# Attention numerators in fp32 column halves, with the last stage written in a new order

## The chip, the cores and the metric

The kernel runs on one core of one Trainium2 chip. The metric is the device time of one execution in microseconds (us). The kernel before takes 759.59 us (median of 3 runs, 759.57 to 759.64).

## The reference

Two branches see the same 2048 rows of x (640 wide): a linear attention with 32 heads of 20 columns, and a feed-forward. A sigmoid gate mixes them row by row.

```
pq, pk = q @ w_phi, k @ w_phi                    # per head
phi = concat(softmax(p), softmax(-p))            # 40 features a head
kv  = phi_k^T v ;  z = sum of phi_k              # over all 2048 rows
num = phi_q kv  ;  den = phi_q z + 1e-6          # per query row and head
a   = concat over heads of (num / den) @ wo
b   = silu(x @ w1) @ w2
out = g * a + (1 - g) * b ,  g = sigmoid(x . gate_w)
```

## The kernel before

The work stands in three stages. The first builds keys, values and the sums kv and z. The second is the feed-forward in four blocks of 512 rows, whose gated result goes to DRAM (`fb_d`). The last stage is the attention of the queries, for eight pairs of query tiles of 128 rows; pairs are numbered by u in the order of the list `PB`.

**Numbers in two parts.** Most products are made in fp32r, a form of fp32 that TensorE takes in one pass at reduced precision. An operand is split into a high part (copy, by ScalarE) and a low part (difference, by VectorE or GpSimd), and a product is three matmuls: high by high, high by low, low by high (`PASSES`).

**One pair of query tiles** goes through these steps; the names are those of the functions.

- `q_mm`: the projection of one tile of 128 queries, 30 matmuls into a PSUM pair `pq`.
- `q_max`, `q_sub` (VectorE): maximum and minimum of each head, and the differences to them, four instructions. `q_exp` (ScalarE): the exponential. `q_sum` (VectorE): the softmax sums. `q_norm` (GpSimd): the product `ez` with z. `q_norm_sum`, `q_small` (VectorE): denominators and the weights of each head. `q_mul` (GpSimd): the features times these weights.
- `t_mm`: the features of both tiles are transposed, in six parts i of 0 to 5, into PSUM tiles `pT`; 22 instructions a pair. `t_hi` (ScalarE) and `t_lo` (VectorE) split each part into `fT`.
- `n_mm`: the numerators, part by part, into PSUM tiles `pn`. Part i holds two groups of three heads (120 features each; part 5 holds the last two heads). Their kv weights lie in `kvw`, 60 columns used of 120, the even group in the left half, the odd in the right, zeros elsewhere; so both groups add up into the same 120 rows of `pn`. Three passes and two groups make 6 matmuls a part, 3 for part 5, 33 a pair. `n_hi` and `n_lo` split `pn` into `oT`.
- `w_mm`: the product with wo, in three turns (two blocks of 128 output columns, two, one) of 16 matmuls a block, into PSUM tiles `pa`. `w_copy` (ScalarE) empties `pa`, `w_add` (GpSimd) adds the feed-forward's part, and a DMA writes it out.

`x_next(k)` prepares k more pieces of x for later projections: ScalarE makes the high part (`xb` from `xrb`), GpSimd the low part. There are three pieces to a pair (512, 512 and 256 columns).

`pT`, `pn` and `pa` share four PSUM tiles in turn (`single`), twelve uses a pair, so each use waits for the reader of the fourth use before it.

**Order.** In the last stage every engine runs its instructions in the order in which the code writes them (`inorder`). `step(u)` for u of 1 to 5 works on pair u, on the projections of two later tiles, b = 2u-1 and c = 2u, and on the wo product of pair u-1. The tile a = 2u-2 is the c of the step before. `last_steps(6)` ends the work. In before, the steps of one pair are interleaved finely: transposes and numerators of single parts alternate, and parts of the wo product stand between them.

Of the kernel before, what the change touches and what calls it, by code (L numbers as in the profile page):

```python
# [30 lines left out]
GW = GR * DH  # L31
NG = H // GR
# [30 lines left out]
def mix_kernel(ctx: ExitStack, tc: tile.TileContext, xT, wqT, wkc, wkr, wv, bd, bdc, cst, wo, w1, w1r, w2, out):  # L63
# [212 lines left out]
    vs = [ta.tile([P, KG, P], F32R, name=f"v{k}")[:, :, :VW] for k in range(VB)]  # L276
# [453 lines left out]
    def wo_load(c):  # L730
        wor_raw[c] = r = raw(f"wo{c}")
        nc.sync.dma_start(r[:GW, :D], wo[c * GW : (c + 1) * GW, :])

    def wo_split(c):
        r = wor_raw.pop(c)
        split(WO[:GW, c, 0], WO[:GW, c, 1], r[:GW, :D])
# [152 lines left out]
    def make_kvw():  # L889

        parts = [w.rearrange("p j f -> p (j f)").rearrange("p (i q f) -> p i q f", q=4, f=KD) for w in kvw]
        for h in range(2):
            nc.gpsimd.memset(parts[h][:, :, 1:3].bitcast(F32), 0.0)  # L893
        pts = []
        for j0, n in ((0, 8), (8, 3)):
            pt = bank(f"pkvt{j0}")
            pts.append((j0, n, pt))
            for j in range(j0, j0 + n):
                w = min(KF, 2 * D - j * KF)
                nc.tensor.transpose(  # L900
                    pt[:w, (j - j0) * KD : (j - j0 + 1) * KD], kvb["kvm"][:, j * KF : j * KF + w], ident[:KD, :KD]
                )
        yield
        for j0, n, pt in pts:
            n = min(n, 2 * NG - j0)
            i0, i1 = j0 // 2, (j0 + n) // 2
            split(
                *(part[:, i0:i1, ::3] for part in parts),
                pt[:GW, : n * KD].rearrange("p (i a f) -> p i a f", a=2, f=KD),
            )  # L910
        split(
            *(kvwr[:, h].rearrange("p (k f) -> p k f", f=REST) for h in range(2)),
            pt[:RC, None, n * KD : n * KD + REST].to_broadcast([RC, KH, REST]),
        )
        yield

    def kvw_of(h, j):
        return kvw[h][:, j, :] if j < 2 * NG else kvwr[:, h, :]

# [77 lines left out]
    def t_hi(u, i):  # L997
        pT = fTs[u, i]
        nj, w = (2, GW) if i < NG else (1, RC)
        if (u, i) < (0, 4):  # L1000
            f = slot(f"fT{u}_{i}")
        else:
            f = slot(f"fT{u}_{i}", fu, "u", 3) if i % 2 == 0 else slot(f"fT{u}_{i}", tb, "fT", 2)
        nc.scalar.copy(f[:w, 0, : nj * 256], pT[:w, : nj * 256])
        fTs[u, i] = f, pT

    def t_lo(u, i):
        f, pT = fTs[u, i]
        nj, w = (2, GW) if i < NG else (1, RC)
        nc.vector.tensor_tensor(  # L1010
            f[:w, 1, : nj * 256], pT[:w, : nj * 256], f[:w, 0, : nj * 256].bitcast(F32), op=ALU.subtract
        )
        fTs[u, i] = f
# [4 lines left out]
    with inorder(PE, DVE, ACT, POOL):  # L1018
# [34 lines left out]
        kvw = [wslot(f"kvw{h}", F32R)[:GW, : 2 * NG * GW].rearrange("p (j f) -> p j f", f=GW) for h in range(2)]  # L1053
        kvwr = fu.tile([RC, 2, GW], F32R, name="kvwr")
# [40 lines left out]
        for i in range(4):  # L1095
            t_mm(0, i, bank)
            t_hi(0, i)
            t_lo(0, i)
# [17 lines left out]
    for k in range(3):  # L1116
        nc.sync.dma_start(wor[k * REST : (k + 1) * REST, :D], wo[NG * GW :, :])

    def n_mm(u, gp, a):
        if (gp, a) == (0, 0):  # L1120
            oTs[u] = tb.tile([GW, 2, NG + 1, 256], F32R, tag="oT", name=f"oT{u}", bufs=2)
# [3 lines left out]
        nj, w = (2, GW) if i < NG else (1, RC)  # L1125
        f = fTs.pop((u, i))
        n = 0
        for jj in range(nj):
            for hk, hp in PASSES:
                nc.tensor.matmul(  # L1130
                    pns[u, gp][:GW, a, :],
                    kvw_of(hk, 2 * i + jj)[:w],
                    f[:w, hp, jj * 256 : (jj + 1) * 256],
                    start=(n == 0),
                    stop=(n == 3 * nj - 1),
                )
                n += 1
# [3 lines left out]
    def n_hi(u, gp):  # L1141
        o, pn = oTs[u], pns[u, gp]
        if gp < 2:
            nc.scalar.copy(o[:, 0, 2 * gp : 2 * gp + 2, :], pn[:GW])
        else:
            nc.scalar.copy(o[:, 0, 4, :], pn[:GW, 0])
            nc.scalar.activation(o[:, 1, 5, :], pn[:GW, 1], AF.Copy, scale=stk[:GW, 0:1])

    def n_lo(u, gp):
        o, pn = oTs[u], pns.pop((u, gp))  # L1150
        k = slice(2 * gp, 2 * gp + 2) if gp < 2 else slice(4, 5)
        nc.vector.tensor_tensor(o[:, 1, k, :], pn[:GW, : k.stop - k.start], o[:, 0, k, :].bitcast(F32), op=ALU.subtract)
        if gp == 2:
            nc.vector.scalar_tensor_tensor(
                o[:, 0, 5, :], pn[:GW, 1], stk[:GW, 1:2], o[:, 1, 5, :].bitcast(F32), op0=ALU.mult, op1=ALU.add
# [4 lines left out]
    def w_mm(u, m0, n):  # L1160
# [9 lines left out]
        for a in range(n):  # L1170
            ds = slice((m0 + a) * P, (m0 + a + 1) * P)
            for k, (c, ho, hw) in enumerate(todo):
                nc.tensor.matmul(  # L1173
                    pa[:, a, :],
                    WO[:GW, c, hw, ds] if c < NG else WOR[:, ds],
                    o[:, ho, c, :],
# [47 lines left out]
    def n_last(u):  # L1224
        n_mm(u, 2, 0)
        n_mm(u, 2, 1)
        n_hi(u, 2)

    def t_pair(u, i):
        for k in (i, i + 1):  # L1230
            t_mm(u, k)
        for k in (i, i + 1):
            t_hi(u, k)

    def n_first(u):
        n_mm(u, 0, 0)
        t_mm(u, 2)
        t_hi(u, 2)
        n_mm(u, 0, 1)
        t_mm(u, 3)  # L1240
        n_hi(u, 0)
        t_hi(u, 3)

    def n_second(u):
        n_mm(u, 1, 0)
        t_mm(u, 4)
        t_mm(u, 5)
        n_mm(u, 1, 1)

    def second_out(u):  # L1250
        t_hi(u, 4)
        t_hi(u, 5)
        n_hi(u, 1)
        t_lo(u, 4)
        t_lo(u, 5)
        n_lo(u, 1)

    def step(u):
        a, b, c = 2 * u - 2, 2 * u - 1, 2 * u
        n_last(u - 1)  # L1260
        t_pair(u, 0)
        n_lo(u - 1, 2)
        if u == 1:
            on(a, lambda t: q_sub(t, 1), q_exp)
        t_lo(u, 0)
        t_lo(u, 1)
        if u == 1:
            on(a, q_norm, q_sum)
            x_next(2)
        on(b, q_mm)  # L1270
        on(a, q_norm_sum)
        if u > 1:
            on(a, q_small)
        n_first(u)
        t_lo(u, 2)
        if u > 1:
            on(b, q_max)
        n_lo(u, 0)
        t_lo(u, 3)
        if u == 1:  # L1280
            on(a, q_small)
            on(b, q_max)
        on(b, lambda t: q_sub(t, 0), lambda t: q_sub(t, 1))
        x_next(3)
        if u > 1:
            on(b, q_exp)
        w_mm(u - 1, 0, 2)
        on(a, q_mul)
        if u == 1:
            w_copy(u - 1, 0)  # L1290
            on(b, q_exp)
        on(b, q_norm)
        n_second(u)
        if u > 1:
            w_copy(u - 1, 0)
        w_add(u - 1, 0)
        if u == 1:
            on(b, q_sum)
        second_out(u)
        if u > 1:  # L1300
            on(b, q_sum)
        on(c, q_mm)
        on(b, q_norm_sum, q_small, q_mul)
        w_mm(u - 1, 2, 2)
        on(c, q_max, lambda t: q_sub(t, 0), lambda t: q_sub(t, 1))
        w_out(u - 1, 2)
        on(c, q_exp)
# [4 lines left out]
    def last_steps(u):  # L1312
        a, b = 2 * u - 2, 2 * u - 1
        n_last(u - 1)
        n_lo(u - 1, 2)
        on(b, q_mm)
        t_pair(u, 0)
        on(a, q_norm_sum)
        on(b, q_max)
        t_lo(u, 0)  # L1320
        on(b, lambda t: q_sub(t, 0))
        t_lo(u, 1)
        w_mm(u - 1, 0, 2)
        on(b, lambda t: q_sub(t, 1))
        w_out(u - 1, 0)
        on(b, q_exp)
        on(a, q_small)
        on(b, q_norm)
        on(a, q_mul)
        on(b, q_sum)  # L1330
        for a in range(2):
            n_mm(u, 0, a)
        for i in (2, 3):
            t_mm(u, i)
        n_hi(u, 0)
# [12 lines left out]
        for k in range(2):
            for i in range(2):
                t_mm(v, i, ks=(k,))  # L1350
        w_copy(u - 1, 4)
        t_hi(v, 0)
        n_mm(u, 2, 0)
        n_mm(u, 2, 1)
        t_lo(v, 0)
        t_hi(v, 1)
        t_lo(v, 1)
        w_add(u - 1, 4)
        n_hi(u, 2)
        n_lo(u, 2)  # L1360
        n_first(v)
        t_lo(v, 2)
        n_lo(v, 0)
        t_lo(v, 3)
        w_mm(u, 0, 2)
        n_second(v)
        w_out(u, 0)
        second_out(v)
        w_mm(u, 2, 2)
        w_out(u, 2)  # L1370
        n_last(v)
        n_lo(v, 2)
        w_mm(u, 4, 1)
        w_out(u, 4)
# [4 lines left out]
    with inorder(PE, DVE, ACT, POOL):  # L1379
        for gp in range(2):  # L1380
            for a in range(2):
                n_mm(0, gp, a)
            n_hi(0, gp)
            n_lo(0, gp)
        for i in (4, 5):
            t_mm(0, i)
            t_hi(0, i)
            t_lo(0, i)
        on(0, q_mm)
        stack(WOR, wor[:GW, :D], raw("wor_h").bitcast(F32R)[:GW, :D], 2)  # L1390
        for p in range(5, 7):
            x_ahead(p)
        x_next(2)
        on(0, q_max, lambda t: q_sub(t, 0))
        for u in range(1, NP - 2):
# [65 lines left out]
```

## Time and profile before

| | |
|---|---|
| median of 3 runs | 759.59 us |
| the profiled execution, its own time | 760.1 us |
| its span, first to last instruction | 758.3 us |
| granted TensorE clock | 0.999 of full speed |
| TensorE busy | 753.5 us, 99% |
| VectorE, ScalarE, GpSimd busy | 371.3, 266.3, 264.4 us |
| last stage, from its first numerator on | 577.33 us to the end, 181.0 us |

The own time of an execution is 1.8 us more than its span. A row of a timeline gives the start, the duration, the engine, the line in the code, what is written from what, and how many instructions were merged; in brackets stands the idle time before it and what ended it. A duration runs from an instruction's start to its result, and the next one of the same engine may start before that, so the pace of a run of equal instructions is read from start to start.

### The profile page before, as it was taken

The page shows a single profiled execution, that of the slowest core. Times are in us where ns is not written, and L with a number is a line of the kernel's source. Part 1 is how long each engine was busy: PE and PEld are TensorE (multiplying, and loading weights), DVE is VectorE, ACT ScalarE, POOL GpSimd, SP SyncE. Part 2 cuts the span into 40 slices and gives each one's busy share as a digit, 9 for nine tenths or more (in the row PEclk, how much of TensorE's full clock was granted, in tenths as well). Part 3 has the DMA queues.
Part 4 walks back from the last instruction along what each step waited for, and adds up shares of the span by engine and source line. Part 5 has one row for each costly group of instructions (what it writes and reads, how often), then busy time and mean ns, then how long its engine had stood idle before and what let it go on. Part 6 is the DMA issues. An engine that isn't in the chain of part 4 may idle for free.

```text
span 758.3 us, 10642 instructions
## 1 busy us (share of the span) xinstructions
PE 753.5 (99%) x4249; PEld 664.2 (88%) x4249; DVE 371.3 (49%) x664; ACT 266.3 (35%) x483; POOL 264.4 (35%) x165
## 2 busy tenths in 40 slices
PE   9999999999999999999999999999999999999998
PEld 7888888888888888888888888888999999999998
DVE  4676666676641221112211122124578888787861
ACT  5444444337541311122111222124354443334341
POOL 2388777768000000000000000000356766855551
PEclk9999999999999999999999999999999999999999
DMA  7111111112650220002200014023003232111222
GB/s 255 53 54 53 53 53 53 60 47 86 206 176 1 69 84 1 1 0 72 84 0 1 1 41 155 9 81 88 2 29 131 93 104 70 55 52 43 70 70 91
DMA packets 35259, 50.17 MB, mean 66 GB/s; under 512 B 3541, under 2 KB 22885, under 8 KB 35210
## 3 DMA queue, kind: packets, MB, share of 16 engines
q1 hardware_dynamic: 35210, 49.50, 20.4%
q8 instruction: 33, 0.54, 0.3%
q14 instruction: 16, 0.13, 0.1%
HBM read 38.37 MB, written 11.11 MB: 65 GB/s over the span
## 4 chain that ended last, share of the span: by engine, by line
PE 97%; DVE 1%; DMA 1%; SPq 0%; ACT 0%; POOL 0%; issue 0%; POOLq 0%; DVEq 0%; ACTq 0%
PE acc L708 25%; PE ph L520 23%; PE kvp L472 16%; PE pq L431 9%; PE pa L1173 9%; PE pn L1130 4%; PE kv L442 2%; PE pT L993 2%; PE kvp L537 2%; PE kvp L330 1%; PE kvq L330 1%; PE pwq L233 1%; PE pwk L319 1%; DMA wvr<-wv 1%; POOL eq L842 0%; PE kvp L453 0%
## 5 line engine op out<-in xcount | busy, mean ns | idle before, releaser
L122 DVE TENSOR_TENSOR u<-ph,u 128x512 fp32r<-128x512 f32 x48 | 33.2, 692 | 187.1 <-ACT u L120 187.1
L708 PE MATMUL acc<-u,w 128*128 128x512 f32 x480 | 114.1, 391 | 0.0
L893 POOL MEMSET kvw<- 120x600 f32 x2 | 1.2, 598 | 319.8 <-PE ph L520 319.8
L708 PEld LDWEIGHTS acc<-u,w 128*128 128x128 f32 x480 | 89.7, 188 | 19.1
L520 PE MATMUL ph<-xf,w 128*128 128x512 f32 x420 | 99.8, 390 | 0.0
L523 ACT ACTIVATE ph<-ph 128x512 f32<-128x512 f32 x48 | 27.9, 582 | 191.2 <-PE ph L520 191.2
L520 PEld LDWEIGHTS ph<-xf,w 128*128 128x128 f32 x420 | 78.7, 188 | 16.7
L472 PE MATMUL kvp<-wh,xa 128*128 128x500 f32 (+1 forms) x420 | 93.1, 357 | 0.0
L472 PEld LDWEIGHTS kvp<-wh,xa 128*128 128x128 f32 x420 | 71.4, 189 | 9.9
L1173 PE MATMUL pa<-oT,wo 120*128 120x256 f32 x600 | 76.6, 280 | 0.0
L1173 PEld LDWEIGHTS pa<-oT,wo 120*128 120x128 f32 x600 | 73.5, 188 | 0.0
L708 PE MATMUL acc<-u,f 128*128 128x512 f32 x300 | 72.3, 392 | 0.0
L520 PE MATMUL ph<-xf,f 128*128 128x512 f32 x300 | 72.3, 392 | 0.0
L520 PEld LDWEIGHTS ph<-xf,f 128*128 128x128 f32 x300 | 56.4, 188 | 12.5
L708 PEld LDWEIGHTS acc<-u,f 128*128 128x128 f32 x300 | 56.2, 188 | 12.1
L806 POOL TENSOR_TENSOR ez<-eq,zbc 128x1280 f32<-128x1280 f32 x16 | 48.2, 3010 | 41.3 <-ACT eq L789 41.2
L122 POOL TENSOR_TENSOR ph<-ek,ph 128x1280 fp32r<-128x1280 f32 x16 | 47.4, 2965 | 27.0 <-ACT ph L120 27.0
L431 PE MATMUL pq<-wq,xb 128*128 128x320 f32 x360 | 55.3, 310 | 0.0
L431 PEld LDWEIGHTS pq<-wq,xb 128*128 128x128 f32 x360 | 52.9, 188 | 0.0
L472 PE MATMUL kvp<-wl,xa 128*128 128x500 f32 (+1 forms) x210 | 47.4, 356 | 0.0
L842 POOL TENSOR_TENSOR eq<-eq,sm 128x1280 f32<-128x1280 f32 x16 | 37.9, 2370 | 15.0 <-DVE sm L836 13.8
L500 POOL TENSOR_TENSOR ek<-ek,st 128x1280 f32<-128x1280 f32 x16 | 38.0, 2372 | 9.1 <-ACT v L290 6.1
(161 smaller groups left out, 1120.0 us busy)
## 6 DMA issues: line engine op xcount, KB each, us to landing
wr<-w SPq DMA_DIRECT2D x26, 320.0 KB, 3.9
xrf<-xT SPq DMA_DIRECT2D x20, 256.0 KB, 3.5
fb_d<-o SPq DMA_DIRECT2D x20, 256.0 KB, 2.4
y<-fb_d SPq DMA_DIRECT2D x16, 256.0 KB, 2.9
out<-y SPq DMA_DIRECT2D x16, 256.0 KB, 2.1
xra<-xT SPq DMA_DIRECT2D x14, 256.0 KB, 3.0
xrb<-xT SPq DMA_DIRECT2D x12, 256.0 KB, 2.7
wvr<-wv SPq DMA_DIRECT2D x5, 321.0 KB, 5.2
```

The costliest lines, as they stand in the source:

```text
L122: eng.tensor_tensor(lo, src, hi.bitcast(F32), op=ALU.subtract)
L330: nc.tensor.matmul(kv_cols(t, lo, hi), x_of(t)[c][:, hx, :], WKV[hw][:, c, lo:hi], start=(opens and hx == 0 and hw == 0), stop=(c == NC - ...
L431: nc.tensor.matmul(dst, xt[c][:, hx, :], w[:, c, hw, lo : lo + n], start=first, stop=(hx == 1 and c == NC - 1))
L472: nc.tensor.matmul(kv_cols(t, lo, hi), xt[c][:, hx, :], WKV[hw][:, c, lo:hi], start=(n == 0), stop=(n == 3 * NC - 1), skip_group_check=True,)
L500: nc.gpsimd.tensor_tensor(groups(e), groups(e), spread(st[:, 1, :]), op=ALU.mult)
L520: nc.tensor.matmul(ph, lhs, rhs, start=(n == 0), stop=(n == len(todo) - 1))
L523: nc.scalar.activation(hs, ph, AF.Silu)
L708: nc.tensor.matmul(acc[m], lhs, rhs, start=(f == order[0] and n == 0), stop=(f == order[-1] and n == len(todo) - 1))
L806: nc.gpsimd.tensor_tensor(ez, Q[t]["e"], zbc, op=ALU.mult)
L842: nc.gpsimd.tensor_tensor(groups(q["e"]), groups(q["e"]), spread(q["sm"][:, 2 * H : 4 * H]), op=ALU.mult)
L1130: nc.tensor.matmul(pns[u, gp][:GW, a, :], kvw_of(hk, 2 * i + jj)[:w], f[:w, hp, jj * 256 : (jj + 1) * 256], start=(n == 0), stop=(n == 3 * ...
L1173: nc.tensor.matmul(pa[:, a, :], WO[:GW, c, hw, ds] if c < NG else WOR[:, ds], o[:, ho, c, :], start=(k == 0), stop=(k == len(todo) - 1),)
```

## The change

The numerators are no longer made in three fp32r passes. The transposed features and `kvw` stay whole in fp32. Part i takes two matmuls: the even group with 64 columns of weights (60 used) into rows 0 to 63 of `pn`, the odd group into rows 64 to 127. Part 5 has halves of 64 and 56 columns. `t_hi` and `t_lo` become one ScalarE copy, `t_out`; the split of `kvw` becomes a copy. The host lays out wo in blocks of 128 rows to match (zeros in the unused rows), and the value tiles `vs` are stored without padding. The functions that ordered the last stage are replaced: all transposes of a pair come in two runs (`t_all`), all its numerators in one (`n_all`).

```
-    vs = [ta.tile([P, KG, P], F32R, name=f"v{k}")[:, :, :VW] for k in range(VB)]
+    vs = [ta.tile([P, KG, VW], F32R, name=f"v{k}") for k in range(VB)]
...
-        split(WO[:GW, c, 0], WO[:GW, c, 1], r[:GW, :D])
+        split(WO[:, c, 0], WO[:, c, 1], r[:, :D])
...
-    def t_hi(u, i):
+    def t_out(u, i):
...
+        f = f.bitcast(F32)
+        nc.scalar.copy(f[:w, : nj * 256], pT[:w, : nj * 256])
-    def t_lo(u, i):
...
     def n_mm(u, gp, a):
...
-        for jj in range(nj):
-            for hk, hp in PASSES:
-                nc.tensor.matmul(
-                    pns[u, gp][:GW, a, :],
-                    kvw_of(hk, 2 * i + jj)[:w],
-                    f[:w, hp, jj * 256 : (jj + 1) * 256],
-                    start=(n == 0),
-                    stop=(n == 3 * nj - 1),
-                )
+        for side in range(2):
+            lhs = kvw_of(i, side)
+            k = side if i < NG else 0
+            nc.tensor.matmul(
+                pns[u, gp][side * CT : side * CT + lhs.shape[-1], a, :],
+                lhs,
+                f[:w, k * 256 : (k + 1) * 256],
+                start=True,
+                stop=True,
+            )
...
     def step(u):
         a, b, c = 2 * u - 2, 2 * u - 1, 2 * u
+        t_all(u, 0, 4)
         if u == 1:
+            on(a, lambda t: q_sub(t, 1), q_exp, q_norm, q_sum)
             x_next(2)
         on(b, q_mm)
+        on(a, q_norm_sum, q_small, q_mul)
+        t_all(u, 4, 6)
+        on(b, q_max, lambda t: q_sub(t, 0), lambda t: q_sub(t, 1), q_exp)
+        x_next(3)
+        w_mm(u - 1, 0, 2)
+        on(b, q_norm, q_sum)
+        w_out(u - 1, 0)
+        n_all(u)
+        n_lo(u, 0)
+        on(b, q_norm_sum, q_small, q_mul)
+        n_lo(u, 1)
+        n_lo(u, 2)
         on(c, q_mm)
         w_mm(u - 1, 2, 2)
+        on(c, q_max, lambda t: q_sub(t, 0), lambda t: q_sub(t, 1), q_exp)
         w_out(u - 1, 2)
         w_mm(u - 1, 4, 1)
         on(c, q_sum, q_norm)
         w_out(u - 1, 4)
```

Three places of the new order, all in the step of pair 3 (its tiles b and c are 5 and 6).

On ScalarE, before: `eq5` and `eq6` are the exponentials of tiles b and c, `xb` the pieces of x, `pac` copies of the wo product.

```order
L120 CAST xb_4_2_5225<-xrb_4_2_4628 128x512
L120 CAST xb_4_4_5230<-xrb_4_4_4923 128x256
L120 CAST xb_5_0_5233<-xrb_5_0_4928 128x512
L789 ACTIVATE eq5_5182<-eq5_5182 128x1280
L1185 COPY pac2_0_5296<-pa2_0_5239 128x512
L1004 CAST fT3_4_5300<-pT3_4_5282 120x512
L1004 CAST fT3_5_5302<-pT3_5_5287 80x256
L1144 CAST oT3_5189<-pn3_1_5275 120x512
L1185 COPY pac2_2_5389<-pa2_2_5352 128x512
L789 ACTIVATE eq6_5342<-eq6_5342 128x1280
```

ScalarE at the same place now, up to the last copy out of the wo product.

```order
L790 ACTIVATE eq5_5099<-eq5_5099 128x1280
L121 CAST xb_4_2_5123<-xrb_4_2_4586 128x512
L121 CAST xb_4_4_5128<-xrb_4_4_4851 128x256
L121 CAST xb_5_0_5131<-xrb_5_0_4856 128x512
L1177 COPY pac2_0_5172<-pa2_0_5136 128x512
L1136 CAST oT3_5176<-pn3_0_5177 128x512
L1136 CAST oT3_5176<-pn3_1_5183 128x512
L1138 CAST oT3_5176<-pn3_2_5189 128x256
L1139 ACTIVATE oT3_5176<-pn3_2_5189,stk_89 120x256
L790 ACTIVATE eq6_5240<-eq6_5240 128x1280
L1177 COPY pac2_2_5281<-pa2_2_5243 128x512
L1177 COPY pac2_4_5307<-pa2_4_5287 128x256
```

The three x pieces moved from ahead of the exponential of tile b to behind it, and the copy `pac2_2` from ahead of the exponential of tile c to behind it.

On GpSimd, before: `eq` rows are `q_mul`, `ez` rows `q_norm`, `y` rows `w_add`.

```order
L122 TENSOR_TENSOR xb_4_2_5225<-xrb_4_2_4628,xb_4_2_5225 128x512
L122 TENSOR_TENSOR xb_4_4_5230<-xrb_4_4_4923,xb_4_4_5230 128x256
L122 TENSOR_TENSOR xb_5_0_5233<-xrb_5_0_4928,xb_5_0_5233 128x512
L842 TENSOR_TENSOR eq4_5041<-eq4_5041,sm4_5039 128x1280
L806 TENSOR_TENSOR ez5_5273<-eq5_5182,zbc_3625 128x1280
L1196 TENSOR_TENSOR y2_0_5237<-pac2_0_5296,y2_0_5237 128x512
L842 TENSOR_TENSOR eq5_5182<-eq5_5182,sm5_5180 128x1280
L1196 TENSOR_TENSOR y2_2_5350<-pac2_2_5389,y2_2_5350 128x512
L806 TENSOR_TENSOR ez6_5414<-eq6_5342,zbc_3625 128x1280
```

GpSimd now.

```order
L843 TENSOR_TENSOR eq4_4969<-eq4_4969,sm4_4967 128x1280
L123 TENSOR_TENSOR xb_4_2_5123<-xrb_4_2_4586,xb_4_2_5123 128x512
L123 TENSOR_TENSOR xb_4_4_5128<-xrb_4_4_4851,xb_4_4_5128 128x256
L123 TENSOR_TENSOR xb_5_0_5131<-xrb_5_0_4856,xb_5_0_5131 128x512
L807 TENSOR_TENSOR ez5_5169<-eq5_5099,zbc_3625 128x1280
L1188 TENSOR_TENSOR y2_0_5134<-pac2_0_5172,y2_0_5134 128x512
L843 TENSOR_TENSOR eq5_5099<-eq5_5099,sm5_5097 128x1280
L1188 TENSOR_TENSOR y2_2_5241<-pac2_2_5281,y2_2_5241 128x512
L807 TENSOR_TENSOR ez6_5305<-eq6_5240,zbc_3625 128x1280
```

The x pieces moved behind the product `eq4`; they now stand directly ahead of `ez5`, which doesn't read them.

On TensorE, before: the first numerators of pair 3, with transposes of the same pair between them.

```order
L1130 MATMUL pn3_0_5190<-fT3_0_5141,kvw0_3844 120x256 x2
L1130 MATMUL pn3_0_5190<-fT3_0_5141,kvw1_3845 120x256
L1130 MATMUL pn3_0_5190<-fT3_0_5141,kvw0_3844 120x256 x2
L1130 MATMUL pn3_0_5190<-fT3_0_5141,kvw1_3845 120x256
L993 MATMUL pT3_2_5197<-ident_81,eq2_4736 120x128 x2
L993 MATMUL pT3_2_5197<-ident_81,eq3_4877 120x128 x2
```

TensorE now: all numerators of pair 3.

```order
L1123 MATMUL pn3_0_5177<-fT3_0_5045,kvw_3844 64x256 x4
L1123 MATMUL pn3_1_5183<-fT3_2_5058,kvw_3844 64x256 x4
L1123 MATMUL pn3_2_5189<-fT3_4_5112,kvw_3844 64x256 x2
L1123 MATMUL pn3_2_5189<-fT3_4_5112,kvwr_3845 64x256
L1123 MATMUL pn3_2_5189<-fT3_4_5112,kvwr_3845 56x256
```

The numerators stand in one run of 12 matmuls and no transposes lie among them.

More of the change, by code (lines that the diff above doesn't have):

```diff
@@ L905, in make_kvw @@
             n = min(n, 2 * NG - j0)
[L906 to L909, printed above, removed]
[L910 to L912 removed]
+            nc.scalar.copy(kvw[:, j0 : j0 + n, :KD], pt[:GW, : n * KD].rearrange("p (j f) -> p j f", f=KD))
+        nc.scalar.copy(
+            kvwr.rearrange("p (k f) -> p k f", f=REST),
             pt[:RC, None, n * KD : n * KD + REST].to_broadcast([RC, KH, REST]),
@@ L1250, in second_out, with t_all, n_all @@
[L1250 to L1256, printed above, removed]
+    def t_all(u, first, last):
+        for i in range(first, last):
+            t_mm(u, i)
+            t_out(u, i)
+    def n_all(u):
+        for gp in range(3):
+            for a in range(2):
+                n_mm(u, gp, a)
+            n_hi(u, gp)
     def step(u):
         a, b, c = 2 * u - 2, 2 * u - 1, 2 * u
-        n_last(u - 1)
-        t_pair(u, 0)
-        n_lo(u - 1, 2)
+        t_all(u, 0, 4)
@@ L1379, in mix_kernel @@
     with inorder(PE, DVE, ACT, POOL):
[L1380 to L1388, printed above, removed]
+        t_all(0, 4, 6)
         on(0, q_mm)
         stack(WOR, wor[:GW, :D], raw("wor_h").bitcast(F32R)[:GW, :D], 2)
+        n_all(0)
         for p in range(5, 7):
```

193 lines of the change are left out of this document (46 added, 147 removed).

## The prediction

> **What bounds the kernel now.** I read the profile's page first, then the timeline of the last stage, then windows of one step each.
>
> ```profile
> PE 753.5 (99%) x4249; PEld 664.2 (88%) x4249; DVE 371.3 (49%) x664; ACT 266.3 (35%) x483; POOL 264.4 (35%) x165
> PE 97%; DVE 1%; DMA 1%; SPq 0%; ACT 0%; POOL 0%; issue 0%; POOLq 0%; DVEq 0%; ACTq 0%
> ```
>
> TensorE (PE) is busy 99% of the span and 97% of the chain that ended last is its own. So the time is TensorE's work, as long as nothing lets it wait. Averages over the span say little about the last stage, so here are three steps of it, each from the first `w_mm` of one pair to that of the next.
>
> ```profile
> 618.42:642.90 24.48, 24.48 (x198) 24.48 (x196) 20.18 (x35) 9.73 (x19) 17.17 (x10) 1.00 0.25 81
> 642.90:667.43 24.53, 24.53 (x198) 24.53 (x197) 19.55 (x33) 9.73 (x19) 17.16 (x10) 1.00 0.19 60
> 667.43:691.97 24.54, 24.54 (x199) 24.54 (x197) 19.46 (x33) 9.32 (x18) 17.12 (x10) 1.00 0.19 59
> ```
>
> The columns are the length, then busy time of TensorE, its weight loads, VectorE, ScalarE and GpSimd, then the granted clock. A step is 24.5 us and TensorE never waits, but VectorE works 19.5 and GpSimd 17.2 of it, handing each tile back and forth. That leaves little room for a worse order.
>
> **TensorE's work.** Paces are read from start to start.
>
> ```profile
> 622.92 0.82 PE L993 MATMUL pT<-ident,eq 128*120 128x128 f32 x6
> 623.50 0.96 PE L1130 MATMUL pn<-fT,kvw 120*120 120x256 f32 x6
> 624.29 4.57 PE L431 MATMUL pq<-wq,xb 128*128 128x320 f32 x30
> 628.70 1.93 PE L1173 MATMUL pa<-oT,wo 120*128 120x256 f32 x15
> 630.59 1.93 PE L1173 MATMUL pa<-oT,wo 120*128 120x256 f32 x15
> L1130 PE MATMUL pn<-fT,kvw 120*120 120x256 f32 x240 | 35.6, 286 | 0.0
> L1130 PE MATMUL pn<-fT,kvwr 80*120 80x256 f32 x24 | 4.2, 283 | 0.0
> ```
>
> Six transposes take 0.58 us, 0.097 each; a projection 4.41; 16 matmuls of the wo product 1.89, 0.118 each. The numerators were 240 + 24 = 264 matmuls, 33 a pair, at the same 256 columns and so the same 0.118: 3.89 us a pair. The change removes these. It adds 12 fp32 matmuls a pair, and what those cost is the first unknown.
>
> ```profile
> 486.85 1.27 PE L233 MATMUL pwq<-constb,wTq 120*128 120x120 f32 x10
> 487.89 3.70 PE L708 MATMUL acc<-u,f 128*128 128x512 f32 x15
> 523.33 1.27 PE L233 MATMUL pwq<-constb,wTq 120*128 120x120 f32 x10
> 524.37 2.54 PE L520 MATMUL ph<-xf,w_r 128*128 128x512 f32 x10
> 526.84 1.30 PE L233 MATMUL pwq<-constb,wTq 40*128 40x40 f32 x10
> 528.07 1.19 PE L708 MATMUL acc<-u,w 128*128 128x512 f32 x4
> L233 PE MATMUL pwq<-constb,wTq 120*128 120x120 f32 x50 | 6.4, 274 | 0.0
> ```
>
> Line 233 is the kernel's other fp32 product. The code issues 25 of this form and the trace has 50, so an fp32 matmul is two instructions, and 12 become 24 a pair. Ten with 120 columns take 1.04 us, 0.104 each. Ten with 40 columns take no less (1.23), so the 128 columns of weights set that pace and the streaming cost is only bounded: at most 0.104 x 256/120 = 0.222 us for 256 columns, and no less than the 0.118 of one fp32r pass. Serially at 0.222 a pair's numerators are 24 x 0.222 = 5.3 us; if the two column halves run side by side, or at the lower pace, 24 x 0.118 = 2.8. I take 2.8, since the row nearest in shape is the 256-column one and the halves use different columns of the array and different rows of PSUM; but no row of this trace shows two halves at once, so 5.3 stays as a rival. The form with 40 rows took 1.23 against 1.04 us, 0.19 more for going to a narrower part of the array and back; I add 0.2 a pair for that: 3.0.
>
> The page "TensorEngine Tiling (Array Packing)" of the Trainium skill, Key Properties, says that different tiles of the array can load weights and multiply in parallel, and that a change of tiling mode drains TensorE. By its first half the numerators cost the 2.8 and the kernel comes to 771 (below), without it 779; its second half agrees in sign with the 0.19 us.
>
> TensorE's step after is thus 24.5 - 3.9 + 3.0 = 23.6 us. VectorE loses `t_lo` and ScalarE little; neither was the bound. The copy instead of the split of `kvw`, and wo in 128 rows, take as many TensorE instructions as before and lie under the feed-forward's matmuls. The unpadded `vs` changes no instruction; I cost it at nothing, plus or minus 1.
>
> **The order: a loop that is longer than the step.** The queues of the order shown above chain the engines together. Let a pass begin with `q_max` of tile b. These rows price its links.
>
> ```profile
> 637.54 0.41 DVE L1152 TENSOR_TENSOR oT<-pn,oT 120x256 fp32r<-120x256 f32 x1
> 638.27 1.28 DVE L1010 TENSOR_TENSOR fT<-pT,fT 120x512 fp32r<-120x512 f32 x2
> 643.72 1.45 ACT L120 CAST xb<-xrb 128x512 fp32r<-128x512 f32 x3
> 644.42 3.25 POOL L122 TENSOR_TENSOR xb<-xrb,xb 128x512 fp32r<-128x512 f32 x3 [4.50 <-ACT xb L120]
> 644.73 0.68 DVE L1152 TENSOR_TENSOR oT<-pn,oT 120x512 fp32r<-120x512 f32 x1
> 645.33 0.68 DVE L1010 TENSOR_TENSOR fT<-pT,fT 120x512 fp32r<-120x512 f32 x1
> 647.50 1.27 ACT L789 ACTIVATE eq<-eq 128x1280 f32<-128x1280 f32 x1 [2.33 <-DVE eq L422]
> 648.68 0.57 ACT L1185 COPY pac<-pa 128x512 f32<-128x512 f32 x1
> 649.95 3.02 POOL L806 TENSOR_TENSOR ez<-eq,zbc 128x1280 f32<-128x1280 f32 x1
> 652.93 1.29 POOL L1196 TENSOR_TENSOR y<-pac,y 128x512 f32<-128x512 f32 x1
> 653.00 1.49 DVE L809 TENSOR_REDUCE sm<-ez 128x64 f32<-128x1280 f32 x1 [0.22 <-POOL ez L806]
> 655.85 0.81 DVE L415 TENSOR_REDUCE mmq<-pq 128x32 f32<-128x640 f32 x1
> 658.88 1.27 ACT L789 ACTIVATE eq<-eq 128x1280 f32<-128x1280 f32 x1 [1.04 <-DVE eq L422]
> ```
>
> - `q_max` and `q_sub` of b until its exponential starts: 655.85 to 658.88, 3.03. The exponential, until the next ScalarE start: 1.18.
> - Now the x pieces stand behind it: the first high part until GpSimd starts 0.70, three low parts 3.25. In before the same 3.25 ran from 644.42, ahead of the exponential at 647.50, while GpSimd had nothing else. That cover is gone.
> - `q_norm` of b until `q_norm_sum` starts 3.05; `q_norm_sum` and `q_small` 2.85.
> - `n_lo` of the second and third group, queued on VectorE ahead of tile c: 0.60 + 0.73.
> - `q_max`, `q_sub`, exponential of c: 3.03 + 1.18.
> - The copy of `pa` (its second turn) is queued on ScalarE behind that exponential, and its `w_add` on GpSimd ahead of `q_norm` of c: 0.57 and a hop of 0.08, then 1.29. In before the copy came ahead of the exponential.
> - `q_norm`, `q_norm_sum`, `q_small` of c: 3.05 + 2.85. Then `q_max` of the next b may start.
>
> The sum is 14.06 + 1.33 + 4.21 + 1.94 + 5.90 = 27.4 us, 3.8 more than TensorE's 23.6. TensorE can't run ahead: `pT` part 2 of the next pair takes the PSUM tile that this copy frees, and part 0 needs `q_mul` of b. So a pass takes 27.4 with three pieces of x, 26.1 with two (one piece of 512 columns, 1.3, less) and 23.5 with none, where TensorE binds again.
>
> **The sum.**
>
> ```profile
> L1004 ACT CAST fT<-pT 120x512 fp32r<-120x512 f32 x40 | 22.5, 595 | 26.3 <-PE pT L993 26.3
> L1147 ACT ACTIVATE oT<-pn,stk 120x256 fp32r<-120x256 f32 x8 | 3.9, 484 | 0.0
> L1146 ACT CAST oT<-pn 120x256 fp32r<-120x256 f32 x8 | 3.0, 374 | 3.8 <-PE pn L1130 3.7
> ```
>
> From the start of the stage (577.33) to the first pass: transposes 0.6, projection 4.4, numerators 3.0, then in one queue on ScalarE the last `n_hi` 0.37 + 0.48, two x copies 1.2, four transposed parts 2.4 and the exponential 1.3, then 3.05 + 2.85: 19.7. Of the 18 pieces 3 are ready earlier and 4 go to the entry, so three passes have three and one has two: 3 x 27.4 + 26.1 = 108.3. The last pass ends at 128.0. There TensorE is ahead by 1.2: after the copy it has 0.4 + 4.4 + 0.6 + hops, 6.0 in all, against 1.29 + 3.05 + 2.85 = 7.2. From 126.8 on it has 320 wo matmuls (37.8), two projections (8.8), 44 transposes (4.3) and three pairs of numerators (9.0), 59.9, and two waits left (the copy ahead of pair 6, about 0.3, and `q_mul` ahead of pair 7, about 1.5): 188.5.
>
> ```profile
> 577.33 3.00 PE L1130 MATMUL pn<-fT,kvw 120*120 120x256 f32 x24
> 754.74 0.28 PE L1173 MATMUL pa<-oT,wor_s 120*128 120x256 f32 x1
> ```
>
> Before, TensorE needed 754.74 + 0.12 - 577.33 = 177.5 for the same. The change adds 11.0 us, some 18 of waits less 8 x 0.9 of work. The profiled execution's 760.1 becomes 771.1; the median was 0.5 under it (759.6), so I forecast 770.6, rounded to **771**.
>
> **Rivals.**
>
> *The halves run one after the other* at 0.222 us. A pair's numerators are 2.5 us longer. Within passes the loop hides this (26.1 against 27.4); at the entry and for the last three pairs it counts, 4 x 2.5 = 10, less 1.8 of waits that vanish: 779. For it: two instructions of one half follow each other in the queue. Against: the second of one half and the first of the other use different columns. Chance 0.27.
>
> *Faster: the loop isn't the bound.* If GpSimd's four terms of a pass (3.25 + 3.05 + 1.29 + 3.05 = 10.6) ran quicker with VectorE relieved of `t_lo`, a pass could fall under TensorE's 23.6. It decides at 3.8 us less, 36% off these terms. Then the time is 759.6 - 8 x 0.9 = 752. Against it:
>
> ```profile
> L806 POOL TENSOR_TENSOR ez<-eq,zbc x16: 2951/3024/3042, 539.3 to 720.2; 128x1280 f32<-128x1280 f32 x16
> ```
>
> Sixteen of them, under light and heavy VectorE load, differ by 3%. Chance 0.06, with 0.02 for ending within 0.2%.
>
> *The clock falls.* TensorE will wait about 3 us at part 2 of each pair, and 1 us just ahead of it, where before it never did.
>
> ```profile
> L299 PE MATMUL warm<-ones 128*128 128x512 f32 x9 | 4.2, 646 | 1.1 <-DVE ones L160 1.1
> L708 PE MATMUL acc<-u,w 128*128 128x512 f32 x480 | 114.1, 391 | 0.0
> ```
>
> After the idle start the same shape took 646 against 391 ns. If 3.4 us of work ran at half pace after each wait, TensorE would lose 1.7 against its lead of 1.2: 0.5 a pass, 2 in all, 773. Chance 0.07. The page "TensorE: Matmul & The Clock Gate" of the Trainium skill, Part 1, says that an idle window of about 3.4 us halves the clock; the forecast waits are just short of that, and the granted 1.00 in all windows above cannot show it.
>
> **Chances and range.** The forecast has 0.58. With numerators cheaper still (weight loads of half the columns) it may be 2 or 3 us less, 768; the serial rival with hops that I missed reaches 782. The range is 768 to 782. Differences within 0.2% (1.5 us) count as the same: faster 0.06, same 0.02, slower 0.92.
>
> **What would show it.** Right: steps of about 27.4 us in the middle of the stage, TensorE waiting at the transposes for `pac` and for `q_mul`, `ez` starting behind the low parts of x, 24 numerators a pair in the trace with starts near 0.118 apart. Starts 0.22 apart mean the serial rival; steps under 24 with no waits, the faster one; a granted clock under 1.00 in the steps, the third. A kernel below 760 would prove the loop wrong.

## The result: 1.6% slower

The changed kernel takes 771.96 us (median of 4 runs, 771.49 to 772.40), the kernel before 759.58 beside it: a ratio of 1.0164 with a 95% interval of 1.0147 to 1.0182. The forecast was 771, in a range of 768 to 782. In the changed kernel the steps have these lines: 990 transposes, 1123 numerators, 432 projections, 1165 the wo product, 416 `q_max`, 790 the exponential, 807 `q_norm`, 810 `q_norm_sum`, 843 `q_mul`, 121 and 123 the two parts of the x pieces, 1177 `w_copy`, 1188 `w_add`.

First the page of the kernel after: busy times, then the chain by engine.

```profile
PE 754.1 (98%) x4177; PEld 650.9 (85%) x4177; DVE 343.9 (45%) x613; ACT 265.2 (34%) x483; POOL 262.4 (34%) x164
PE 79%; POOL 9%; DVE 6%; issue 4%; ACT 1%; POOLq 0%; DVEq 0%
```

TensorE was 97% of the chain and is now 79%; GpSimd and VectorE, together 1% before, hold 15%. TensorE's busy time did not fall although 72 instructions went; the paragraph on the clock below says why. The windows, from the numerators of one pair to those of the next, with the same columns as before, say where the time lies.

```profile
598.66:629.62 30.96, 26.31 (x187) 24.23 (x186) 19.00 (x30) 10.81 (x19) 19.23 (x11) 0.89 0.22 72
629.62:655.47 25.85, 23.93 (x188) 22.42 (x187) 16.14 (x26) 8.44 (x18) 17.08 (x10) 1.00 0.24 77
655.47:684.11 28.64, 25.57 (x188) 23.83 (x187) 16.59 (x27) 10.91 (x20) 17.01 (x10) 0.94 0.16 52
614.80:616.40 1.60, 1.51 (x6) 1.13 (x6) 1.60 (x3) 0.00 (x0) 0.03 (x1) 0.50 0.07 25
645.50:647.50 2.00, 1.93 (x15) 1.94 (x16) 1.07 (x1) 2.00 (x6) 1.91 (x2) 1.00 0.00 0
672.70:674.70 2.00, 1.92 (x9) 1.93 (x10) 1.08 (x1) 1.81 (x5) 1.90 (x2) 0.50 0.00 0
```

Three steps average 28.5 us where three took 24.5 before, and TensorE idles 1.9 to 4.7 us in each. In two of the three the granted clock is under 1.00: the last three rows show 0.50 behind the waits of the first and third step and 1.00 behind that of the second.

The timeline of after, one whole pass of the loop and the starts of the others:

```profile
579.47 0.82 PE L990 MATMUL pT<-ident,eq 128*120 128x128 f32 x6
584.62 2.38 PE L1123 MATMUL pn<-fT,kvw 120*64 120x256 f32 x20
587.36 1.55 PE L990 MATMUL pT<-ident,eq 128*120 128x128 f32 x12
598.29 0.82 DVE L416 TENSOR_REDUCE mmq<-pq 128x32 f32<-128x640 f32 x1
625.46 0.81 DVE L416 TENSOR_REDUCE mmq<-pq 128x32 f32<-128x640 f32 x1
645.57 1.09 PE L990 MATMUL pT<-ident,eq 128*120 128x128 f32 x8 [1.92 <-ACT pac L1177]
652.69 0.81 DVE L416 TENSOR_REDUCE mmq<-pq 128x32 f32<-128x640 f32 x1
655.73 1.27 ACT L790 ACTIVATE eq<-eq 128x1280 f32<-128x1280 f32 x1 [3.35 <-DVE eq L423]
657.59 3.24 POOL L123 TENSOR_TENSOR xb<-xrb,xb 128x512 fp32r<-128x512 f32 x3 [2.30 <-ACT xb L121]
660.79 2.95 POOL L807 TENSOR_TENSOR ez<-eq,zbc 128x1280 f32<-128x1280 f32 x1
663.78 1.49 DVE L810 TENSOR_REDUCE sm<-ez 128x64 f32<-128x1280 f32 x1 [3.75 <-POOL ez L807]
670.98 1.27 ACT L790 ACTIVATE eq<-eq 128x1280 f32<-128x1280 f32 x1 [10.54 <-DVE eq L423]
672.16 0.84 ACT L1177 COPY pac<-pa 128x512 f32<-128x512 f32 x2
672.78 1.96 PE L990 MATMUL pT<-ident,eq 128*120 128x128 f32 x8 [2.64 <-ACT pac L1177]
672.80 1.27 POOL L1188 TENSOR_TENSOR y<-pac,y 128x512 f32<-128x512 f32 x1 [3.59 <-ACT pac L1177]
674.03 2.93 POOL L807 TENSOR_TENSOR ez<-eq,zbc 128x1280 f32<-128x1280 f32 x1
679.84 0.81 DVE L416 TENSOR_REDUCE mmq<-pq 128x32 f32<-128x640 f32 x1
705.78 0.81 DVE L416 TENSOR_REDUCE mmq<-pq 128x32 f32<-128x640 f32 x1
766.28 0.28 PE L1165 MATMUL pa<-oT,wor_s 120*128 120x256 f32 x1
```

This is the loop of the prediction, link by link: exponential of b at 655.73, three low parts of x from 657.59, `ez` of b only when they are through (660.79), `q_norm_sum` at 663.78. Then the exponential of c at 670.98, the copy of `pa` behind it at 672.16, TensorE's transposes released by that copy at 672.78 after 2.64 us idle, `w_add` ahead of `ez` of c, and the next pass at 679.84. Passes take 27.17, 27.23, 27.15 and 25.94 us. The 24 numerators of a pair (20 on `kvw`, 4 on `kvwr`) take 587.36 - 584.62 = 2.74 us, 0.114 each on average. The view of waits, for the stage, gives TensorE's idle time by what ended it (total, times, longest):

```profile
PE pT L990 <- ACT pac L1177: 7.1, 4, 2.6
PE pT L990 <- POOL eq L843: 2.7, 3, 1.4
```

Both waits are the ones that were forecast.

### The profile page after: what moved, and what is told of

Its sections match the earlier page's. It is cut to its first block, busy times and chain, and to the rows that moved or that the text cites. A ratio compares the mean times of both kernels' runs of the same rounds, so it can differ in the third digit from the quotient of the medians.

```text
span 769.8 us, 10451 instructions
## 1 busy us (share of the span) xinstructions
PE 754.1 (98%) x4177; PEld 650.9 (85%) x4177; DVE 343.9 (45%) x613; ACT 265.2 (34%) x483; POOL 262.4 (34%) x164
## 4 chain that ended last, share of the span: by engine, by line
PE 79%; POOL 9%; DVE 6%; issue 4%; ACT 1%; POOLq 0%; DVEq 0%
PE acc L709 25%; PE ph L521 23%; PE kvp L473 16%; POOL ez L807 5%; PE pq L432 3%; POOL eq L843 3%; PE pa L1165 3%; DVE sm L810 2%; PE kv L443 2%; PE kvp L538 2%; PE kvp L331 1%; PE kvq L331 1%; POOL xb L123 1%; PE pwk L320 1%; PE pwq L234 1%
## 5 line engine op out<-in xcount | busy, mean ns | idle before, releaser
L1165 PE MATMUL pa<-oT,wo 128*128 128x256 f32 x600 | 77.8, 283 | 0.0
L1165 PEld LDWEIGHTS pa<-oT,wo 128*128 128x128 f32 x600 | 74.6, 189 | 0.8 <-ACT oT L1136 0.8
L709 PE MATMUL acc<-u,f 128*128 128x512 f32 x300 | 72.3, 392 | 0.0
L521 PE MATMUL ph<-xf,f 128*128 128x512 f32 x300 | 72.3, 392 | 0.0
L807 POOL TENSOR_TENSOR ez<-eq,zbc 128x1280 f32<-128x1280 f32 x16 | 47.4, 2960 | 42.3 <-ACT eq L790 42.3
L432 PE MATMUL pq<-wq,xb 128*128 128x320 f32 x360 | 57.1, 316 | 0.0
L123 POOL TENSOR_TENSOR ph<-ek,ph 128x1280 fp32r<-128x1280 f32 x16 | 47.5, 2967 | 27.4 <-ACT ph L121 27.4
L790 ACT ACTIVATE eq<-eq 128x1280 f32<-128x1280 f32 x16 | 20.4, 1277 | 85.5 <-DVE eq L423 85.5
```

The source lines that it names most:

```text
L123: eng.tensor_tensor(lo, src, hi.bitcast(F32), op=ALU.subtract)
L432: nc.tensor.matmul(dst, xt[c][:, hx, :], w[:, c, hw, lo : lo + n], start=first, stop=(hx == 1 and c == NC - 1))
L521: nc.tensor.matmul(ph, lhs, rhs, start=(n == 0), stop=(n == len(todo) - 1))
L709: nc.tensor.matmul(acc[m], lhs, rhs, start=(f == order[0] and n == 0), stop=(f == order[-1] and n == len(todo) - 1))
L790: nc.scalar.activation(Q[t]["e"], Q[t]["e"], AF.Exp)
L807: nc.gpsimd.tensor_tensor(ez, Q[t]["e"], zbc, op=ALU.mult)
```

## Experiments

The theory was that two placements make the loop: the x pieces ahead of `ez` of b on GpSimd, and the copy of `pa` behind the exponential of c. Its rivals: slower TensorE work, and the clock.

**x_ahead**: the x pieces ahead of `q_mul`, where before had them.

```
         on(b, q_mm)
+        x_next(3)
         on(a, q_norm_sum, q_small, q_mul)
         ...
-        x_next(3)
```

> The changed kernel with one line moved: in step(u) the x pieces (x_next(3)) stand ahead of q_norm_sum of tile a instead of behind the exponential of tile b. Loop theory: a pass of 27.2 us loses 0.70 + 3.25 and comes to 23.3, under TensorE's 23.6, so TensorE binds from the second step on: three passes give back about 3.5 each, the fourth about 2, the entry about 1, so 758 to 760 us. Rival, that the fp32 numerators and the clock took the time and the order only spread it: 770 to 772 as it is.

758.39 us (758.03 to 759.86), ratio to before 0.9985 (0.9976 to 0.9994). One moved line takes away 13.6 us, more than the 12.4 that were lost. `q_max` of b in its timeline:

```profile
622.07 0.81 DVE L416 TENSOR_REDUCE mmq<-pq 128x32 f32<-128x640 f32 x1
645.54 0.81 DVE L416 TENSOR_REDUCE mmq<-pq 128x32 f32<-128x640 f32 x1
669.06 0.81 DVE L416 TENSOR_REDUCE mmq<-pq 128x32 f32<-128x640 f32 x1
```

A pass is 23.5 us, the prediction's figure for a loop with none of the pieces. TensorE doesn't wait in these passes; its own step, from the numerators of one pair to the next, is 23.7 here.

**copy_ahead**: the copy of `pa` ahead of the exponential of c.

```
-        on(c, q_max, lambda t: q_sub(t, 0), lambda t: q_sub(t, 1), q_exp)
+        on(c, q_max, lambda t: q_sub(t, 0), lambda t: q_sub(t, 1))
         w_out(u - 1, 2)
+        on(c, q_exp)
```

> The changed kernel with the copy and addition of the wo product's second turn (w_out(u - 1, 2)) ahead of the exponential of tile c. Loop theory: a pass loses the copy 0.65 and w_add 1.29, 27.2 to 25.3, in four passes, so 764 to 765 us, with TensorE's wait for pac at part 2 gone and one for the next copy (pa of the third turn) in its place. Rival, that the wait for pac is by itself the cost and not a link of a loop: the waits for pac in the trace vanish whole and 7 us of idle come back plus the clock, 761 to 763. Rival, that the order isn't the cause: 770 to 772.

765.64 us (765.49 to 765.99), ratio 1.0079 (1.0064 to 1.0094): 6.3 us less than after, but 0.6 over what I expected. The timeline shows the pass that gave less:

```profile
598.08 0.81 DVE L416 TENSOR_REDUCE mmq<-pq 128x32 f32<-128x640 f32 x1
618.70 6.30 PE L432 MATMUL pq<-wq,xb 128*128 128x320 f32 x30
625.03 0.82 DVE L416 TENSOR_REDUCE mmq<-pq 128x32 f32<-128x640 f32 x1 [1.45 <-PE pq L432]
650.50 0.81 DVE L416 TENSOR_REDUCE mmq<-pq 128x32 f32<-128x640 f32 x1
```

The second pass is 25.5 us, the 27.4 less the copy's links of 1.94, and the third the same. The first is 26.95: its projection took 6.30 us, where the one quoted with the prediction took 4.57, because the granted clock had fallen after a string of waits (0.50 from 618 to 622), and `q_max` waited 1.45 for it. The clock rival thus costs where TensorE's lead is used up.

**both_ahead**: both moves.

> Both moves in one kernel. Loop theory: the pass is 21.3 us, well under TensorE's 23.6; what is left is the entry and the waits of the first step, so 754 to 757 us, less than either alone and less than the kernel before. Rival (numerators and clock): 770 to 772.

757.40 us (757.15 to 757.73), ratio 0.9970 (0.9958 to 0.9982), a little above what I expected. With no loop left, two steps of the timeline are TensorE's own:

```profile
648.13 2.38 PE L1123 MATMUL pn<-fT,kvw 120*64 120x256 f32 x20
671.83 2.38 PE L1123 MATMUL pn<-fT,kvw 120*64 120x256 f32 x20
```

A step is 23.70 us against 24.5 before. The moves overlap: 13.6 and 6.3 alone, 14.6 together, since below 23.7 TensorE binds.

**old_order**: the new numerators in the old order, with the `t_lo` calls left out. If only the order were to blame, this had to be the gain alone.

> The numerators of the change (fp32, two column halves) in the order of the kernel before, with the low parts of the transposes left out since they are not needed. If the numerators by themselves gain 3.9 - 2.9 us a pair and the order lost it all, the kernel takes 8 x 1.0 less than before: 751 to 753 us with TensorE still busy without waits. If fp32 numerators cost more where they stand between other work (the array goes to halves and back four or five times a pair instead of once, 0.2 each): up to 759. Rival, that the numerators are the cost: 765 or more.

763.35 us (763.18 to 763.50), ratio 1.0049 (1.0032 to 1.0065). This is 10 us over what I expected and 4 over its upper alternative, and TensorE waits only 0.2 us in the stage. Its timeline of TensorE, where numerators and transposes alternate:

```profile
667.52 0.65 PE L1123 MATMUL pn<-fT,kvw 120*64 120x256 f32 x4
668.11 0.65 PE L990 MATMUL pT<-ident,eq 128*120 128x128 f32 x4
668.69 0.65 PE L1123 MATMUL pn<-fT,kvw 120*64 120x256 f32 x4
```

Four numerators take 0.59 us here and four transposes 0.58; at their paces in long runs they would take 0.46 (4 x 0.114) and 0.39 (4 x 0.097). Going from column halves to the whole array and back costs 0.32 us where transposes stand on both sides. The old order does it at five places of a step, the new one at one. By the Trainium skill, "TensorEngine Tiling (Array Packing)", Key Properties, a change of tiling mode drains TensorE; these rows agree and give the price.

The other part of the miss stands in the groups of the feed-forward stage, far ahead of the change. Here they are in the kernel after.

```profile
L709 PE MATMUL acc<-u,w 128*128 128x512 f32 x480 | 115.2, 393 | 0.0
L521 PE MATMUL ph<-xf,w 128*128 128x512 f32 x420 | 100.6, 392 | 0.0
```

Before, the first of these groups (line 708 there, quoted with the prediction's clock rival) held 114.1 us. So the matmuls that read the weight tiles `w` took 1.1 us more; the 300 on the same line that read the tiles `f` held 72.3 in both. The diff doesn't touch either. But it makes the tile `kvwr` one copy wide instead of two, 480 bytes instead of 960 a partition, and what is allocated behind it moves. I tested this by giving the width back.

**after_pad**, **both_pad**, **old_order_pad**: after, both_ahead and old_order with `kvwr` as wide as before.

```
-        kvwr = fu.tile([RC, GW], F32, name="kvwr")
+        kvwr = fu.tile([RC, 2, GW], F32, name="kvwr")[:, 0]
```

> The changed kernel with kvwr as a tile of twice the width again (half of it unused), so that every tile that lies behind it in memory, the feed-forward's weights of the pool fp among them, has the address of before. In the changed kernel the feed-forward reaches its last matmul 2.1 us later than before (579.2 against 577.1 in the two traces), with 393 instead of 389 ns in the median of the matmuls on those weights. If the address did it: the last feed-forward matmul is back at 577.1 and the time falls by 2 us, to 770. If it is the unpadded vs or anything else of the change: it stays at 579 and 772.

> Both moves (x pieces ahead, copy ahead) and the wide kvwr. If the address cost is 2.1 us wherever it stands: 757.4 less 2.1, 755.3, the fastest version so far and under before by 0.6%. If not, 757.4.

> The numerators of the change in the order of before, with the wide kvwr. Takes the address cost from old_order: 763.35 less 2.1, 761.2. What is left over the kernel before (759.6) is then the price of going between halves and the whole array: the trace of old_order has 4 numerators start to start in 0.585 us instead of 0.457 and 4 transposes behind them in 0.58 instead of 0.39, five such places a pair, some 1.6 us a pair, against the 1.15 that the numerators gain.

770.06 us (770.01 to 770.39), ratio 1.0137 (1.0123 to 1.0150); 754.41 (754.12 to 754.58), ratio 0.9929 (0.9916 to 0.9941); 760.16 (759.68 to 760.54), ratio 1.0005 (0.9996 to 1.0014). So 1.9, 3.0 and 3.2 us hang on the place of tiles alone. In the groups of after_pad the two that read `w` take 1.1 and 0.8 us less again:

```profile
L709 PE MATMUL acc<-u,w 128*128 128x512 f32 x480 | 114.1, 392 | 0.0
L521 PE MATMUL ph<-xf,w 128*128 128x512 f32 x420 | 99.8, 391 | 0.0
```

Where TensorE binds the last stage too, more comes back: in the timelines a block of the wo product takes 1.91 us with the narrow `kvwr` and 1.89 with the wide one, which is 0.8 over 40 blocks. And with the place put right, the numerators in the old order gain nothing: what they gain goes into the changes between halves and whole array. In the last stage TensorE begins a run of numerators 35 times in old_order_pad and 8 times in both_pad. Without its waits the stage takes 177.5 us in the one, as in before, and 170.0 in the other, so each further run costs 0.28. Both_pad has the gain, because all numerators of a pair stand in one run. Two steps of its timeline are 23.60 us apart:

```profile
645.62 2.38 PE L1123 MATMUL pn<-fT,kvw 120*64 120x256 f32 x20
669.22 2.38 PE L1123 MATMUL pn<-fT,kvw 120*64 120x256 f32 x20
```

**vs_wide**, **kvwr_512**: both_pad with the padded value tiles of before, and with `kvwr` 512 bytes wide.

```
-    vs = [ta.tile([P, KG, VW], F32R, name=f"v{k}") for k in range(VB)]
+    vs = [ta.tile([P, KG, P], F32R, name=f"v{k}")[:, :, :VW] for k in range(VB)]
```

```
-        kvwr = fu.tile([RC, 2, GW], F32, name="kvwr")[:, 0]
+        kvwr = fu.tile([RC, GW + 8], F32, name="kvwr")[:, :GW]
```

> The version with both moves and the wide kvwr, and the value tiles vs stored with padding again, as before the change. If the unpadded vs is worth nothing, as the prediction put it, 754.4 us, the same as without this edit. The rival is the bound of plus or minus 1 us: 753.4 or 755.4, shown then by other durations of the matmuls in the key and value stage.

> The version with both moves, with kvwr 512 bytes wide instead of 960 (754.4 us) or 480 (757.4 us). If the tiles behind kvwr are read slower because 480 bytes bring them off a multiple of 64 bytes, 512, which is such a multiple as 960 is, gives 754.4. If it takes another distance (a multiple of 192 or 320, or a place that only the 960 happens to give), 757.4 or something between.

754.20 us (753.88 to 754.39), ratio 0.9927 (0.9913 to 0.9940), and 753.79 (753.76 to 756.25), ratio 0.9929 (0.9917 to 0.9942). The padding of `vs` is worth nothing. In time 512 bytes serve as well as 960; 480 don't. But two groups of kvwr_512 show that they get there differently:

```profile
L709 PE MATMUL acc<-u,w 128*128 128x512 f32 x480 | 113.6, 390 | 0.0
L1165 PE MATMUL pa<-oT,wo 128*128 128x256 f32 x600 | 77.9, 283 | 0.0
```

The feed-forward's 113.6 us is less than with 960 bytes (114.1), and the wo product's 77.9 is what 480 bytes give (77.8), not 960 (76.9). The multiple of 64 bytes that I had in mind fits the feed-forward and not the wo product. The place of tiles is shown to matter; the rule stays open.

**halves_apart**: both_ahead, with the even groups of two parts first and then their odd groups, so that two matmuls in a row use the same half.

```
-    (in words) part 0: even half, odd half; part 1: even half, odd half
+    (in words) even half of part 0, even half of part 1, odd half of part 0, odd half of part 1
```

> Both moves, and the same numerators with their matmuls in another order: of each two parts first both even groups (column half 0), then both odd ones (half 1), so that neighbours in the queue mostly use the same half. Theory, that the two halves of a part run side by side (24 instructions in 2.74 us, 0.114 each, while one alone takes 0.379 against 0.283 for an fp32r matmul of the same 256 columns, so 0.096 longer, about one more streaming of the 256 columns): one after the other they need about 0.21 each, 5 us a pair, and TensorE is the bound here, so 8 x 2.2, about 774 us. Rival, that an fp32 instruction streams once at 0.114 and halves don't matter: no change, 757 to 758.

757.56 us (757.26 to 757.99), ratio 0.9971 (0.9960 to 0.9981), as both_ahead. The time is the rival's, and in the timeline the 24 take no longer:

```profile
648.10 2.43 PE L1129 MATMUL pn<-fT,kvw 120*64 120x256 f32 x20
650.31 0.66 PE L1129 MATMUL pn<-fT,kvwr 80*64 80x256 f32 x4
```

20 in 2.21 us, 0.110 each. But the second row doesn't fit the rival. One of these instructions lasts 0.38 us from start to result, so if the four started 0.110 apart they would fill 0.71 us. They fill 0.66. In the kernel after, the timeline from 587.22 on, where only the last two numerators of a run are left, shows it more plainly:

```profile
587.05 0.39 PE L1123 MATMUL pn<-fT,kvwr 80*64 80x256 f32 x2
```

Two instructions of 0.38 us, one of each half, in 0.39 together: they start within 0.01 of each other. Of the 192 numerators of after, 96 start within 0.02 us of another.

**four_times**: both_pad, each numerator matmul issued four times in a row, so that 7 of 8 neighbours are of one half.

```
+            for _ in range(4):
                 nc.tensor.matmul(...)
```

> both_pad with each numerator matmul issued four times in a row (the same result four times), so that eight instructions in a row use the same column half: 96 instructions a pair instead of 24. If a half alone runs at the pace seen so far: 0.114 each, 72 x 0.114 x 8 = 66 us more, about 820. If two different halves side by side make that pace and one alone needs 0.21: 96 x 0.21 less the overlap at the seams, some 17 us a pair more than now, about 890.

825.94 us, one run: 71.5 more than both_pad for 576 more instructions, 0.124 each, near the 820 of the first alternative. But the timeline doesn't bear out its reason, that one half alone runs at 0.114. The end of a run in it (the last row is what is left from 649.3 on):

```profile
647.29 0.43 PE L1124 MATMUL pn<-fT,kvwr 80*64 80x256 f32 x1
647.50 0.38 PE L1124 MATMUL pn<-fT,kvw 120*64 120x256 f32 x1
647.56 0.38 PE L1124 MATMUL pn<-fT,kvwr 80*64 80x256 f32 x1
647.72 0.38 PE L1124 MATMUL pn<-fT,kvw 120*64 120x256 f32 x1
647.77 0.38 PE L1124 MATMUL pn<-fT,kvwr 80*64 80x256 f32 x1
649.12 1.03 PE L1124 MATMUL pn<-fT,kvwr 80*56 80x256 f32 x4
```

Here the rows on `kvw` are of the odd half and stand ahead of those on `kvwr`, of the even half, in the code. TensorE starts them in turn all the same (on TensorE the order of the code holds within a half alone): each half keeps its own pace of 0.21 to 0.22, and the two go on at once. The last row has the odd half alone, when nothing of the even half is left: four instructions of 0.38 us fill 1.03, so they start 0.22 apart. So one half by itself needs about 0.22 an instruction, and 0.11 is two halves side by side. This is the theory of halves_apart. What failed there and here was only its consequence, that neighbours of one half in the queue would run one after the other: the other half's instructions don't wait for them.

**whole_width**: the kernel before with fp32 numerators over its 120 columns, 11 matmuls (22 instructions) a pair, `t_lo` left out.

```
-            for hk, hp in PASSES:
-                nc.tensor.matmul(..., kvw_of(hk, 2 * i + jj)[:w], f[:w, hp, ...])
+            nc.tensor.matmul(..., kvw_of(2 * i + jj)[:w], f[:w, ...])
```

> The kernel before, its order and its 120-row layout, with fp32 numerators over the whole width: the two groups of a part still add up into the same 120 rows, each with its 120 columns of weights (half of them zeros), one fp32 matmul a group instead of three fp32r passes; t_lo and the split of kvw go, the address of the other tiles is kept. 11 fp32 matmuls are 22 instructions a pair. If an fp32 instruction streams its 256 columns at the same pace whatever its width (0.114): 22 x 0.114 = 2.5 us a pair against 3.9 and no change between halves and the whole array, so 8 x 1.4 less: 748 to 750, the fastest. If over the whole width it needs two streamings (0.213 to 0.222) and the column half is what makes it quick: 4.8 us a pair, 766 to 768.

765.93 us (765.85 to 766.04), ratio 1.0080 (1.0062 to 1.0098). In the timeline:

```profile
668.35 1.03 PE L1123 MATMUL pn<-fT,kvw 120*120 120x256 f32 x4
669.21 0.60 PE L992 MATMUL pT<-ident,eq 128*120 128x128 f32 x4
```

Four instructions take 0.86 us, 0.215 each: 22 of them are 4.7 us against 3.89 for the three fp32r passes, and 8 x 0.84 = 6.7 is near the 6.2 measured. That is the pace of one half alone (0.22): an instruction costs the same with 120 columns of weights as with 64 or 56. So fp32 is cheap here only because two halves run at once.

## Why the prediction was right

**The numerators: value and reason right.** 2.8 us was forecast and 2.74 measured. Of the two reasons that the prediction gave for it, "the two column halves run side by side" is what the traces show: the halves start 0.01 us apart (after), go on at once in whatever order they are queued (halves_apart, four_times), and one alone takes 0.22 an instruction. The rule on tiles in parallel (the Trainium skill, "TensorEngine Tiling (Array Packing)", Key Properties) holds in these traces. The other reason, "at the lower pace", failed: no fp32 instruction of 256 columns ran at 0.118 by itself. The upper bound of 0.222 was nearly exact, 0.215 in whole_width; the prediction took it for loose because it read the 128 columns of weights as the limit of line 233. But 0.104 for 120 columns is the pace of 0.215 for 256, so the streaming set it. The serial rival, in which the halves follow each other at 0.222, is excluded. The sign "starts near 0.118 apart" was too coarse: it holds for the average alone.

**The loop** was right in each link and a little long: passes of 27.2 and 25.9 us against 27.4 and 26.1. x_ahead and copy_ahead each took out the links they were meant to and brought the 23.5 and the 25.5 that the sum gives. From the end of the feed-forward (579.47) to the first pass (598.29) it took 18.8 against 19.7, the four passes 107.5 against 108.3, and the rest, to 0.12 behind the last start at 766.28, 60.6 against 188.5 - 128.0 = 60.5. The stage is 186.9 against 188.5: 9.4 us over the 177.5 of before where I had 11.0.

**The address term was missing.** The stage starts 579.47 - 577.33 = 2.1 us later. I costed the layout at nothing plus or minus 1 and looked at `vs`, which is worth nothing; what moved was the place of the tiles behind `kvwr`. 9.4 + 2.1 = 11.5 is the difference of the spans (769.8 against 758.3). That the forecast landed within 1 us is luck: a stage 1.6 too long stood against this 2.1.

**The steps and the waits.** TensorE's own step of 23.6 us is that of both_pad (23.60). TensorE's waits for `pac` came to 7.1 us over four where I had about 3 each, those for `q_mul` to 0.9 each where I had 1. GpSimd, relieved of `t_lo` beside it, didn't save the faster rival: its 16 `ez` take 2960 ns against 3010 in before, 2%, not 36%.

**The clock** did fall, which I gave 0.07, but cost after nothing: passes with and without a fall are 27.2. The sum had TensorE ahead by 1.2 and charged 0.5 a pass beyond that; the slow projections stayed within the lead. They do show in TensorE's busy time: transposes hold 24.1 us and projections from `xb` 57.1 in after, 20.4 and 55.9 in both_ahead, which has under 2 us of waits. This, with the address, is much of why the busy time didn't fall, and part of why the sum's 18 us of waits are only 11.4 us of idle time. Copy_ahead, whose passes are shorter, shows the price: 1.5 us once.

From the runs, then: the change without the two placements and the address, that is fp32 numerators in one run and the rest of the new order, is 754.41 - 759.85 = -5.4 us (759.85 is the kernel before beside these runs); the two placements +15.65 (770.06 - 754.41); the address +1.9. Together +12.1.

## What to carry to other kernels

When an order is written anew, follow each queue between a hand-off and its use: the x pieces ahead of one product and a copy behind one exponential turned a gain of 5 us into a loss of 10. Batch what uses the array in another shape, since each change costs. After a tile changes size, compare the durations of matmuls that the diff doesn't touch.

## What the runs showed that was not expected

- A tile of 480 bytes a partition in place of 960 costs 1.9 to 3.2 us of 760, in matmuls on tiles that lie elsewhere (480 of them 1.1 us longer). With 512 bytes the time is that of 960, but other matmuls are fast and slow.
- An fp32 instruction streams 256 columns in 0.215 us, with 120 columns of weights or with 64 or 56. Two on different column halves run at once, 0.11 each, and matmuls of one half start ahead of earlier ones of the other.
- Going between column halves and the whole array and back costs 0.32 us between transposes, 0.28 on average over the stage.
- The granted clock fell to 0.50 after waits of 1.26 and 1.41 us with 0.4 us of work between, and it was 0.50 again at 672.70 after waits of 0.43 and 2.64, but 1.00 after a lone wait of 1.92. The page "TensorE: Matmul & The Clock Gate" of the Trainium skill, Part 1, has an idle window of some 3.4 us for that. Here it was 0.50 at 614.80, 3.0 us after the first of these waits began at 611.81 and with work in between, so the measurement differs: shorter waits were enough. How they add up isn't shown.
